# Forty unused matrix products behind the last product of a fused attention and token-mixer kernel

## The chip, the cores and the metric

The kernel runs on one core of one Trainium2 chip. The metric is the device time of one launch in microseconds, as the median of several executions. One further execution was recorded by the hardware profiler, and every row of a profile in this document comes from such a recorded execution. The engines are named as the profile names them: PE is TensorE (PEld its weight loads), DVE is VectorE, ACT is ScalarE, POOL is GpSimd, SP is SyncE. A "q" behind an engine's name marks its sequencer, which waits, branches and issues while the engine itself does no arithmetic.

## The reference

For x of 2048 tokens by 512 channels the kernel computes `g * a + (1 - g) * b`, where

- g is the sigmoid of the token's dot product with `gate_w`,
- a is softmax attention with 32 heads of 16 channels each (projections `wqkv` and `wo`),
- b is a mixer block across tokens: layer norm, `w1` (2048 to 1792), bias, gelu, `w2` (1792 to 2048), bias.

All values are float32.

## The kernel before, in words

The work has stages. First x is turned and split into two parts of reduced precision (a high and a low part, type fp32r), and the queries, keys and values are projected. Then comes the mixer's first layer. Then a long stage does the attention for 32 groups of heads; the mixer's second layer and most of the output projection are done in the same stage, product by product between the attention's products.

Three shapes of product on the array matter here.

- A score product (line 804, `s<-qs,ks`) uses 64 of the array's 128 rows and all 128 columns, with 512 moving columns, in fp32r. Two of them, one on each half of the rows, are issued next to each other.
- A value product (line 768, `av<-pt,v`) uses 128 rows and 17 columns, with 256 moving columns, in float32. Its output lies at partition 0, 32, 64 or 96, so four of them lie beside each other in the array's columns.
- The products of the output projection (line 887, `pa<-wo,o`) use 96 or 128 rows and all 128 columns, with 512 moving columns, in fp32r.

The last stage (lines 874 to 948) finishes eight tiles of the output. It has one PSUM bank for each tile, `pa[0]` to `pa[7]`, and runs in an order that is written out by hand (`manual_schedule`): each engine executes its instructions in the order of the code. The last pair of heads is normalised on DVE (`sums`, `hi`, `lo`, lines 903 to 910). TensorE then multiplies it into the even tiles (`last_pair(0, ...)`, line 917), then into the odd ones, and completes tiles 3, 5 and 7 with `others(*LATE)` (line 887). `finish(t, queue)` (lines 928 to 931) lets DVE add a finished bank to its row of the output, and lets SP or ACT store the row:

```python
        last_pair(1, parts, LATE)
        others(*LATE)
        for t, queue in ((1, nc.sync), (3, nc.scalar), (5, nc.sync), (7, nc.scalar)):
            finish(t, queue)
    end_ctx.close()
    att_ctx.close()

    far_off = nc.values_load(flag, min_val=0, max_val=H, skip_runtime_bounds_check_because="a count")
    with tc.If(far_off != 0):
```

Behind this stage every engine loads one number, `flag`, from memory into a register of its own sequencer (line 953), and branches on it (line 954). With these inputs the flag is zero, so every engine jumps over a long block that computes attention in a safer way. At the jump's target each engine waits for its own outstanding work, signals that it has arrived, and POOL collects these signals and releases all of them again; that is the end of the program (the rows of line 1027). In SP's list at the target stand waits for all transfers and for the other engines' counts.

The order of TensorE's instructions at the end is therefore: the products of line 917 for the odd tiles, twelve products of line 887, the load of the flag, the branch, and at its target the wait for its own products and the signal.

Of the kernel before, what the change touches and what calls it, by code (L numbers as in the profile page):

```python
# [21 lines left out]
P = 128  # L22
# [8 lines left out]
NB = 512  # L31
NQ = S // NB
VC = DH + 1
# [12 lines left out]
HALF = 64  # L46
# [12 lines left out]
def gated_mix(ctx: ExitStack, tc: tile.TileContext, a_x, a_wqkv, a_wo, b_w1, b_b1, b_w2, b_b2, gate_w, out):  # L59
    nc = tc.nc  # L60
# [277 lines left out]
    with tc.tile_pool(name="ln0", bufs=3, side="right") as ln:  # L338
# [18 lines left out]
        for b in range(ND):  # L357
# [9 lines left out]
            for n in range(NQ):  # L367
# [5 lines left out]
                if n % 2 == 0:  # L373
                    c = 2 * b + n // 2
# [39 lines left out]
    with tc.tile_pool(name="ln1", bufs=3, side="right") as ln, tc.tile_pool(name="gl", bufs=2, side="right") as gl:  # L414
# [29 lines left out]
        for f0, cs in order.items():  # L444
            n = min(NB, F - f0) // P
# [74 lines left out]
    QC = NB // 2  # L520
# [17 lines left out]
    def second_layer(t):  # L538

        box = []  # L540

        def step(fc, k):
            if fc == 0 and k == 0:
                box.append(ps_dn.tile([P, D], F32, name="dn"))
            if fc % 4 == 0 and k == 0:
                load_weight()
                box.append(ready.pop(0))
            at = slice(fc % 4 * P, (fc % 4 + 1) * P)
            hi, lo = (w[:, at] for w in box[-1])
            a, b = ((hi, u_hi), (hi, u_lo), (lo, u_hi))[k]  # L550
            last = fc == NF - 1 and k == 2
            return box[0], a, b[:, fc, :], fc == 0 and k == 0, last, (lambda: second_out(t, box[0])) if last else None

        return [(step, fc, k) for fc in range(NF) for k in range(3)]
# [59 lines left out]
    def o_matmuls(half, t, n, m):  # L614

        cols = slice(t % 8 * P, (t % 8 + 1) * P)
        for i in range(n, m):
            k, j = divmod(i, 3)
            hi, lo = (x[:, cols] for x in o_parts[half, k])
            a, b = ((hi, wo_hi), (hi, wo_lo), (lo, wo_hi))[j]  # L620
            yield a, b[: a.shape[0], k, :]
# [40 lines left out]
    def put(steps, at, sizes):  # L662
        for n in sizes:
            dense[at] = [steps.pop(0) for _ in range(n)]
            at += 1
        assert not steps
        return at
# [4 lines left out]
    def put_outputs(tiles, n, m, at, sizes=None):  # L672
        for t in tiles:
            steps, load = project(t, n, m)
            call(at - 1, load)
            at = put(steps, at, sizes or [m - n])
        return at

    def sizes_of(at, n, fours):

        sizes = [6] * n
        for i in [i for i in reversed(range(n)) if (at + i) % TWOS][:fours]:
            sizes[i] = 4
        return sizes
# [6 lines left out]
    first, at = steps[:28], put(steps[28:], 0, [8, 6])  # L691
    for t in range(NS):
        if t:
            at = put(second_layer(t), at, sizes_of(at, 9, 6) if t > 9 else sizes_of(at, 8, 3))
        if t == 7:
            call(at - 8, fetch_o, 0, 0)
            call(at - 5, fetch_o, 0, 1)
            at = put_outputs(range(NH), 0, 6, at)
        if t == 10:
            call(at - 8, fetch_o, 0, 2)  # L700
            call(at - 5, fetch_o, 0, 3)
            at = put_outputs(range(NH), 6, 12, at)
# [4 lines left out]
    at = put_outputs(range(NS - 3, NS), 0, 4, at)  # L707
    assert at == (NP + 12) * TWOS + 7
    call(at - 3, fetch_o, 1, 2)
    at = put_outputs(range(NH, NS - 3), 0, EARLY, at, [4, 4])  # L710
    at = put_outputs(range(NS - 3, NS), 4, EARLY, at)
# [9 lines left out]
    def column_halves(x):  # L721
        x = x.rearrange("p (i m c) -> p m i c", i=2, m=2)
        return x[:, 0], x[:, 1]
# [57 lines left out]
    with tc.manual_schedule(engines=engines):  # L781
# [3 lines left out]
        for n, (step, *args) in enumerate(first):  # L785
            if n and n % 12 == 0:
                split_weight(nc.vector.tensor_copy, nc.vector.tensor_tensor)
            ps, a, b, start, stop, done = step(*args)
# [27 lines left out]
        for grp in range(NG):  # L816
            at = [0, 0]
            for ph in range(2 * TWOS + 1):
# [45 lines left out]
                n = 2 if ph == 2 * TWOS and grp < NG - 1 else len(late)  # L864
# [8 lines left out]
    with (  # L873
        tc.tile_pool(name="ps_end", bufs=1, space=PSUM, reuse_waits="tile") as ps_end,
        tc.manual_schedule(engines=engines),
    ):
        pa = [ps_end.tile([P, D], F32, name=f"pa{t}") for t in range(8)]


        LATE = 3, 5, 7  # L880

        def others(*tiles, m=0, n=3 * ND):

            for t in tiles:
                mms = list(enumerate(o_matmuls(1, NH + t, EARLY, 3 * ND)))
                for i, (a, b) in mms[m:n]:
                    nc.tensor.matmul(pa[t], a, b, start=i == 0 and t not in LATE, stop=i == len(mms) - 1 and t in LATE)  # L887

        tiles = [end.tile([P, NB], dt, name=name) for name, dt in (("sums", F32), ("hi", F32R), ("lo", F32R))]
        sums, hi, lo = (column_halves(x) for x in tiles)  # L890
        last = column_halves(last_ot)
        totals = [column_halves(pa[t])[0] for t in (5, 7)]
        others(0, n=3)
        nc.tensor.matmul(totals[0], sums_of, last[0], start=True, stop=True)  # L894
        nc.tensor.matmul(totals[1], sums_of, last[1], start=True, stop=True)  # L895
        others(0, m=3)
        others(2, 4, 6)

        def low(m):
            nc.vector.tensor_tensor(lo[m], sums[m], hi[m].bitcast(F32), ALU.subtract)  # L900


        nc.vector.reciprocal(sums[0], totals[0])
        nc.vector.tensor_mul(sums[0], last[0], sums[0])
        nc.scalar.copy(hi[0], sums[0])
        nc.vector.reciprocal(sums[1], totals[1])
        low(0)
        nc.vector.tensor_mul(sums[1], last[1], sums[1])
        nc.vector.tensor_copy(hi[1], sums[1])
        low(1)  # L910

        def last_pair(m, parts, late=()):
            for n, (a, b) in enumerate(parts):
                for i in range(2):
                    for j in range(4):
                        t, at = 2 * j + m, slice(32 * j, 32 * j + DH)
                        nc.tensor.matmul(  # L917
                            pa[t],
                            a[m][at, i, :],
                            wq[b][at, i, :],  # L920
                            start=n == i == 0 and t in late,
                            stop=n == 2 and i == 1 and t not in late,
                        )

        def row_of(t):
            return rows[NH + t], g[:, NH + t : NH + t + 1], of[(NH + t) * P : (NH + t + 1) * P, :]

        def finish(t, queue):
            row, gate, dst = row_of(t)
            nc.vector.scalar_tensor_tensor(row, pa[t], gate, row, ALU.mult, ALU.add)  # L930
            queue.dma_start(dst, row)

        def scaled(t):
            res = end.tile([P, D], F32, name=f"res{t}")
            nc.scalar.activation(res, pa[t], AF.Copy, scale=row_of(t)[1])
            nc.gpsimd.tensor_tensor(row_of(t)[0], res, row_of(t)[0], ALU.add)

        parts = [(hi, 0), (hi, 1), (lo, 0)]
        last_pair(0, parts)
        others(1)  # L940
        scaled(2)
        for t, queue in ((0, nc.sync), (4, nc.scalar), (6, nc.sync)):
            finish(t, queue)
        nc.scalar.dma_start(row_of(2)[2], row_of(2)[0])
        last_pair(1, parts, LATE)
        others(*LATE)
        for t, queue in ((1, nc.sync), (3, nc.scalar), (5, nc.sync), (7, nc.scalar)):
            finish(t, queue)
    end_ctx.close()
    att_ctx.close()  # L950

# [2 lines left out]
    with tc.If(far_off != 0):  # L954
        with (
# [6 lines left out]
            for b in range(ND):  # L962
                with tc.For_i(0, P // DH, 1) as hi:
# [7 lines left out]
                    for t in range(NS):  # L971
# [4 lines left out]
                        m = pool.tile([P, 1], F32, name="m")  # L976
# [7 lines left out]
                        for n in range(NQ):  # L984
                            tp = ps_t.tile([P, NB // P, P], F32, name="tp")
                            for i in range(NB // P):
                                c = n * (NB // P) + i
# [3 lines left out]
                            for i in range(NB // P):  # L991
                                c = n * (NB // P) + i
                                nc.tensor.matmul(po, pt[:, i, :], vh[:, c, 0, :], start=c == 0, stop=c == NS - 1)
                        nc.vector.tensor_scalar_mul(og[:, t, ds(hi * DH + b * P, DH)], po, l)
            for t in range(NS):
# [6 lines left out]
                pa = ps_o.tile([P, NB], F32, name="po")  # L1002
# [28 lines left out]
```

## Time and profile before

| | us |
|---|---|
| median of 3 executions | 1308.36 (1308.08 to 1308.73) |
| the profiled execution, whole | 1307.55 |
| its span, from the first to the last instruction | 1305.8 |
| TensorE busy in the span | 1299.0 |
| start of the last product | 1299.79 |
| start of the last store's issue | 1300.99 |

A row of the timeline gives the start in microseconds from the start of the span, the duration, the engine, the source line, the operation, what it writes and reads, the shape (rows times columns of the array, then partitions times elements) and the number of instructions that are merged in the row. A row of the view of one source line gives the engine, the operation, the count, the least, median and greatest duration in nanoseconds, and the starts of the first and the last of them, to a tenth of a microsecond. A row of the chain of waits gives start and duration of one link. A row of the transfer queues gives packets, megabytes, and the time that the packets took as a share of sixteen engines over the window asked for, so that share times sixteen times the window is that time.

### The profile page before, as it was taken

The numbers are of one execution on the slowest core, as the hardware profiler recorded it, in microseconds if no ns is written. First come the engines' busy times: TensorE is split into PE (matmuls) and PEld (weight loads), VectorE is DVE, ScalarE is ACT, GpSimd is POOL, SyncE is SP. The second block draws the span as 40 slices with busy tenths as digits, with TensorE's granted clock in tenths as the row PEclk, the third lists the DMA queues.
The fourth block names the chain that finished last, engine by engine and source line by source line (L and its number), as shares of the span: only waits on it lengthen the run. The fifth ranks groups of instructions, "written<-read, shape, count | busy, mean of one in ns | idle before, by whom it ended". The sixth has DMA issues, their size and how long they took to land.

```text
span 1305.8 us, 32289 instructions
## 1 busy us (share of the span) xinstructions
PE 1299.0 (99%) x13282; PEld 764.3 (59%) x13282; DVE 403.9 (31%) x538; ACT 1090.6 (84%) x1248; POOL 200.0 (15%) x467
## 2 busy tenths in 40 slices
PE   9999999999999999999999999999999999999998
PEld 7888888886555555555555555555555555454444
DVE  5775361445121111122322111232111111233324
ACT  3443343448999999999999999999999999999994
POOL 0210244453101011011000111100010101100000
PEclk9999999999999999999999999999999999999999
DMA  4497643337443333334655443545433333365522
GB/s 129 144 308 275 229 117 97 97 88 148 75 86 66 62 75 84 69 75 90 126 113 121 82 76 72 120 115 118 79 67 63 74 62 77 75 123 115 112 64 74
DMA packets 93384, 138.41 MB, mean 106 GB/s; under 512 B 14293, under 2 KB 53355, under 8 KB 90156
## 3 DMA queue, kind: packets, MB, share of 16 engines
q1 hardware_dynamic: 92652, 135.20, 44.3%
q8 instruction: 107, 1.75, 0.6%
q10 hardware_dynamic: 576, 1.05, 0.2%
q14 instruction: 49, 0.40, 0.1%
HBM read 99.63 MB, written 36.56 MB: 104 GB/s over the span
## 4 chain that ended last, share of the span: by engine, by line
PE 99%; DVE 0%; issue 0%
PE av L768 37%; PE s L804 29%; PE acc L412 12%; PE acc L73 10%; PE dn L844 10%; PE pa L887 1%; PE acc L184 1%; PE dn L789 0%; PE acc L251 0%; PE acc L228 0%; PE pa L917 0%; DVE base L930 0%; PE pa L895 0%; PE pa L894 0%; DVE idle L223 0%; PE acc L210 0%
## 5 line engine op out<-in xcount | busy, mean ns | idle before, releaser
L813 ACT ACTIVATE pt<-s 128x1024 f32<-128x1024 f32 x1024 | 962.5, 1025 | 20.9 <-PE s L804 14.9
L804 PE MATMUL s<-qs,ks 64*128 64x512 f32 x2048 | 521.3, 420 | 0.0
L768 PE MATMUL av<-pt,v 128*17 128x256 f32 x8192 | 510.6, 381 | 0.0
L804 PEld LDWEIGHTS s<-qs,ks 64*128 64x128 f32 x2048 | 297.6, 184 | 207.6 <-ACT pt L813 182.8
L768 PEld LDWEIGHTS av<-pt,v 128*17 128x17 f32 x8192 | 205.3, 97 | 259.5 <-issue 119.2
L844 PE MATMUL dn<-u_hi,w_hi 64*128 64x512 f32 x428 | 179.6, 420 | 0.0
L844 PE MATMUL dn<-u_hi,w_lo 64*128 64x512 f32 x430 | 170.2, 396 | 0.0
L844 PE MATMUL dn<-u_lo,w_hi 64*128 64x512 f32 x430 | 170.1, 396 | 0.0
L66 POOL TENSOR_TENSOR w_lo<-w_raw,w_hi 128x512 fp32r<-128x512 f32 (+1 forms) x126 | 151.7, 1205 | 115.1 <-ACT w_hi L65 108.5
L848 POOL MEMSET token<- 1x1 f32 x320 | 29.9, 93 | 873.3 <-PE dn L844 704.1
L731 DVE COPY ot<-av 128x512 f32<-128x512 f32 x31 | 21.5, 692 | 344.9 <-PE av L768 344.9
L65 ACT CAST w_hi<-w_raw 128x512 fp32r<-128x512 f32 (+1 forms) x67 | 38.1, 569 | 79.6 <-PE acc L412 58.8
L742 DVE RECIPROCAL rt<-rt 128x512 f32<-128x512 f32 x31 | 104.0, 3353 | 1.1
L412 PE MATMUL acc<-h_hi,w_hi 128*128 128x512 f32 x224 | 87.1, 389 | 0.0
L412 PE MATMUL acc<-h_lo,w_hi 128*128 128x512 f32 x224 | 87.1, 389 | 0.0
L412 PE MATMUL acc<-h_hi,w_lo 128*128 128x512 f32 x224 | 87.1, 389 | 0.0
L65 DVE CAST w_hi<-w_raw 128x512 fp32r<-128x512 f32 (+1 forms) x61 | 23.5, 387 | 190.2 <-PE s L804 82.0
L844 PEld LDWEIGHTS dn<-u_lo,w_hi 64*128 64x128 f32 x430 | 79.5, 185 | 2.5 <-POOL token L848 0.2
L844 PEld LDWEIGHTS dn<-u_hi,w_lo 64*128 64x128 f32 x430 | 79.4, 185 | 2.6
L844 PEld LDWEIGHTS dn<-u_hi,w_hi 64*128 64x128 f32 x428 | 78.8, 184 | 2.2
L73 PE MATMUL acc<-xt_hi,wc_hi 128*128 128x512 f32 x128 | 49.8, 389 | 0.0
L73 PE MATMUL acc<-xt_lo,wc_hi 128*128 128x512 f32 x128 | 49.8, 389 | 0.0
(142 smaller groups left out, 1001.5 us busy)
## 6 DMA issues: line engine op xcount, KB each, us to landing
w_raw<-in_B_w_dram SPq DMA_DIRECT2D x96, 256.0 KB
ks<-kp SPq DMA_DIRECT2D x192, 128.0 KB
qs<-qp SPq DMA_DIRECT2D x256, 64.0 KB
qp<-pc SPq DMA_DIRECT2D x16, 768.0 KB
x<-in_A_x_dram SPq DMA_DIRECT2D x32, 256.0 KB
kp<-pc SPq DMA_DIRECT2D x16, 512.0 KB
w_raw<-in_B_w_dram SPq DMA_DIRECT2D x32, 128.0 KB
bp<-row SPq DMA_DIRECT2D x16, 256.0 KB
```

Of the source, the lines that this page charges most:

```text
L65: copy(hi, src)
L66: return sub(lo, src, hi.bitcast(F32), ALU.subtract)
L73: nc.tensor.matmul(ps, a, b, start=start and n == 0, stop=stop and n == last)
L184: nc.tensor.transpose(turns[t][:, k, :], xs[t][:, k * P : (k + 1) * P], ident)
L412: nc.tensor.matmul(p, a, b, start=first and k == 0, stop=last and k == 2)
L731: nc.vector.tensor_copy(ot, av)
L742: nc.vector.reciprocal(rt, rt)
L768: nc.tensor.matmul(av[32 * j : 32 * j + VC, i * QC : (i + 1) * QC], v[:, c, g % NP * 2 + i, :], pt[:, h * QC : (h + 1) * QC], start=added[ ...
L804: nc.tensor.matmul(s[:, m, :], kt[grp][rows, c * P : (c + 1) * P], qt[grp][rows, qb * NB : (qb + 1) * NB], start=True, stop=True,)
L813: nc.scalar.activation(pt, s, AF.Exp, scale=SCALE)
L844: mm = nc.tensor.matmul(ps, a[half], b[half], start=first and not second, stop=last and bool(second))
L848: fence = nc.gpsimd.memset(token, 0.0)
```

## The change

Behind the last `finish` of the last stage, and still inside its hand-written order, the changed kernel issues forty products. They read `sums`, `hi` and `lo`, which the stage has left in memory, and write the banks `pa[0]` and `pa[4]`, whose tiles have been read by DVE by then. Nothing reads what they write.

```diff
         for t, queue in ((1, nc.sync), (3, nc.scalar), (5, nc.sync), (7, nc.scalar)):
             finish(t, queue)
+        sums_t, parts_t = tiles[0], tiles[1:]
+        free = pa[0], pa[4]
+        def tile_of(r, c, rows_n, cols_n, n, a, b, m=None):
+            at = slice(r * rows_n, (r + 1) * rows_n)
+            m = m or cols_n
+            nc.tensor.matmul(
+                free[r][c * cols_n : c * cols_n + m, :n], a[at, c * cols_n : c * cols_n + m], b[at, :n], start=True, stop=True
+            )
+        def rounds(count, nr, n_cols, n, a, b, m=None):
+            for _ in range(count):
+                for c in range(n_cols):
+                    for r in range(nr):
+                        tile_of(r, c, P // nr, P // n_cols, n, a, b, m)
+        def score_slots(n):
+            rounds(n, 2, 1, NB, *parts_t)
+        def v_blocks(n, nr):
+            rounds(n, nr, 4, QC, sums_t, sums_t, VC)
+        score_slots(2)
+        v_blocks(1, 2)
+        score_slots(2)
+        v_blocks(1, 1)
+        v_blocks(1, 2)
+        score_slots(1)
+        for _ in range(2):
+            tile_of(0, 0, HALF, P, NB, *parts_t)
+            for c in range(4):
+                tile_of(1, c, HALF, 32, QC, sums_t, sums_t, VC)
     end_ctx.close()
     att_ctx.close()
```

`P` is 128, `HALF` 64, `NB` 512, `QC` 256 and `VC` 17. `score_slots(n)` issues n pairs of the score shape, one product on each half of the rows. `v_blocks(1, 1)` issues four products of the value shape; `v_blocks(1, 2)` issues eight, which use 64 rows each, so that the array is cut into two by four tiles. The last loop puts one product of the score shape on the upper half of the rows, and four of the value shape on the lower half, twice. Twelve products have the score shape and 28 a value shape. On TensorE the forty stand between the last product of line 887 and the load of the flag. The instructions of the other engines and their order are what they were.

## The prediction

> **What bounds the kernel now.** I read the page first, for the share of TensorE; then the last links of the chain of waits; then the timeline of the last microseconds; and last the views of the source lines 953, 954 and 1027, because behind the last product no engine is busy any more and the page shows nothing there. From the page and the chain:
>
> ```profile
> span 1305.8 us, 32289 instructions
> ...
> PE 1299.0 (99%) x13282; PEld 764.3 (59%) x13282; DVE 403.9 (31%) x538; ACT 1090.6 (84%) x1248; POOL 200.0 (15%) x467
> ```
>
> ```profile
> 1297.19 3.00 PE pa L887 x12
> 1300.19 0.02 issue
> 1300.21 0.75 DVE base L930
> ```
>
> TensorE is busy for 99% of the span, so forty more products look like forty more on the path. But the chain ends with a DVE row at 1300.96, and the span ends at 1305.8: for 4.8 us nothing is computed. What ends last there is not in the chain, which follows busy engines only. The timeline has the last product and the last store:
>
> ```profile
> 1299.79 0.39 PE L887 MATMUL pa<-wo_hi,o_lo 96*128 96x512 f32 x1
> ...
> 1300.99 0.34 ACTq L931 DMA_DIRECT2D out_dram<-base  x1
> ```
>
> The views of lines 953, 954 and 1027 have the sequencers:
>
> ```profile
> L953 PEldq TENSOR_LOAD <-flag x1: 772/772/772, 1296.1 to 1296.1; - x1
> ```
>
> ```profile
> L954 SPq EVENT_SEMAPHORE  x8: 17/17/17, 1303.8 to 1304.4; - x8
> ...
> L954 PEldq COMPARE_BRANCH  x1: 5028/5028/5028, 1297.0 to 1297.0; - x1
> L954 DVEq COMPARE_BRANCH  x1: 76/76/76, 1300.8 to 1300.8; - x1
> L954 SPq COMPARE_BRANCH  x1: 45/45/45, 1301.1 to 1301.1; - x1
> L954 ACTq COMPARE_BRANCH  x1: 54/54/54, 1301.9 to 1301.9; - x1
> L954 PEldq EVENT_SEMAPHORE  x1: 51/51/51, 1302.1 to 1302.1; - x1
> L954 DVEq EVENT_SEMAPHORE  x1: 21/21/21, 1304.2 to 1304.2; - x1
> L954 ACTq EVENT_SEMAPHORE  x1: 17/17/17, 1304.8 to 1304.8; - x1
> ```
>
> ```profile
> L1027 SPq DRAIN  x3: 7/7/7, 1305.0 to 1305.3; - x3
> L1027 POOLq EVENT_SEMAPHORE  x4: 17/17/17, 1305.0 to 1305.7; - x4
> ...
> L1027 PEldq DRAIN  x2: 8/8/8, 1302.2 to 1305.3; - x2
> ...
> L1027 ACTq DRAIN  x2: 8/8/8, 1304.9 to 1305.3; - x2
> ```
>
> The reader is to see four things. The jump costs DVE 1300.9 to 1304.2, SP 1301.1 to 1303.8 and ACT 1302.0 to 1304.8, that is 2.7 to 3.3 us each. The arrivals at the end (each engine's first DRAIN) are ACT's at 1304.9 and SP's at 1305.0; POOL collects them at 1305.0 and the span ends 0.8 us later. TensorE arrives at 1302.2, so it has **2.8 us of slack**. And its sequencer loads the flag at 1296.1, far ahead of the last product: the load does not wait for the array.
>
> **The change part by part.** Nothing is removed, and the other engines keep their instructions. So there is no mechanism for a gain; what is added stands on TensorE alone, and counts only as far as its arrival comes after 1305.0.
>
> *The array's time.* A float32 product counts twice: the code issues 4096 value products and the page has
>
> ```profile
> L768 PE MATMUL av<-pt,v 128*17 128x256 f32 x8192 | 510.6, 381 | 0.0
> ```
>
> So the 12 score products are 12 passes and the 28 value products 56, 68 in all. From the chain, then the timeline:
>
> ```profile
> 1283.48 1.42 PE av L768 x24
> 1284.90 0.66 PE s L804 x4
> ```
>
> ```profile
> 1287.42 0.13 PEld L768 LDWEIGHTS av<-pt,v 128*17 128x17 f32 x8 [0.50 <-ACT pt L813]
> 1287.97 0.19 PEld L887 LDWEIGHTS pa<-wo_hi,o_lo 128*128 128x128 f32 x1 [0.42 <-issue]
> ```
>
> Four score products cost 0.66 us with the change of tiling behind them, two I take at half, 0.33. Eight value passes cost 0.55 up to the next shape; 24 cost 1.42, so four more cost (1.42 - 0.55) / 4 = 0.22, and the change of tiling about 0.55 - 2 x 0.22 = 0.11. Four value passes at a time is what this rate means, since one lasts 381 ns. The value shape on half the rows is in no row. Bound from below: eight at a time, as column tiles run four at a time and row halves two at a time, 0.55 for its 16 passes. Four at a time would be 0.55 + 2 x 0.22 = 0.99. From above: one after another, 16 x 0.22 + 0.11 = 3.63. I take eight at a time, because both ways of sharing are in the two rows. In order: 0.66 (4 passes), 0.55 (16), 0.66 (4), 0.55 (8), 0.55 (16), 0.33 (2), and twice 0.33 + 0.55 (9 each), **5.06 us**; four at a time 5.94. It starts at 1299.79 + 0.22 + 0.11 = 1300.12 and ends at 1305.2 (1306.1). The first two products wait until DVE has read `pa[0]` and `pa[4]`, the first two of
>
> ```profile
> 1294.61 2.06 DVE L930 SCALAR_TENSOR_TENSOR base<-pa,g,base 128x512 f32<-128x512 f32 x3
> ```
>
> which is done by 1294.61 + 2/3 x 2.06 = 1296.0; the wait costs nothing, and only TensorE's own work is queued behind it. If the array were all that counts, TensorE would arrive at 1305.3 and cost 0.3.
>
> *The sequencer's time.* The forty stand ahead of the flag's load, and behind the load come the jump and the arrival. How far ahead of the array does the sequencer get? At the load, 1296.1, these were still to come or running (busy time of one window, the count in brackets, then a row of the timeline):
>
> ```profile
> 1296.11:1300.40 4.29, 4.06 (x32) 1.00 0.94 334
> ```
>
> ```profile
> 1296.55 0.64 PE L917 MATMUL pa<-wq,lo 16*128 16x512 f32 x8
> ```
>
> At most 32 passes, at least these 8 and the 12 of line 887: 20 to 32, and I take 24. So with 68 added the load is reached when about 44 have started, 48 and 36 at the ends. All three lie in the fifth block (passes 33 to 48), which opens at 1300.12 + 0.66 + 0.55 + 0.66 + 0.55 = 1302.54. The 44th is in its second group: **1302.8** (four at a time: 1303.4). [...]
>
> *The jump.* From load to branch is 1297.0 - 1296.1 = 0.9. The branch took 5.0 on TensorE, against 2.7 to 3.3 elsewhere. The transfer queues tell why: three windows, 1297.3 to 1297.4, 1299.6 to 1299.7 and, for DVE, 1301.9 to 1302.1, hold the start of one fetch of instructions each.
>
> ```profile
> q8 instruction: 1, 0.02, 63.4%
> ```
>
> ```profile
> q8 instruction: 1, 0.02, 59.4%
> ```
>
> ```profile
> q14 instruction: 1, 0.01, 23.9%
> ```
>
> Share times 16 times window: 1.01, 0.95 and 0.76 us. DVE's fetch starts 1.0 us after its branch, and DVE goes on 1304.2 - 1302.7 = 1.5 after the fetch. TensorE's second fetch ends at 1300.6 and it goes on 1.4 later, at 1302.0: that is the target's. It starts 2.6 after the branch, not 1.0, because, as I read it, an ordinary fetch was under way until 1298.3. In the changed kernel that ordinary fetch comes at the same place in the code, 136 instructions ahead of the new place of the jump, and is long over. So the branch costs 1.0 + 0.95 + 1.4 = **3.4**; SP's 2.7 is the end below, 5.0 the end above.
>
> *The sum.* Load 1302.8, branch 1303.7, target 1307.1, signal 0.1 later 1307.2, end 0.8 later 1308.0. Against 1305.8 that is **2.2 us** later. The profiled execution is 1307.55 us long, 1.75 more than its span; with 2.2 it would be 1309.8. It lies 0.8 under the median, and the difference carries over: 1308.36 + 2.2 = **1310.6 us**. With four at a time 2.8 us and 1311.2; with a branch of 2.7, 1.5 us and 1309.9.
>
> **The rivals.**
>
> *The tail hides it.* If the sequencer can run much further ahead than 24, the jump is over before the array is done: 0.3 us, 1308.7 (1.2 us and 1309.6 with four at a time). For it: no row shows a limit. Against it: 20 to 32 at a moment when it had no wait left to hold it. 0.12.
>
> *The jump costs 5.0 again: slower.* If the long branch is a property of TensorE, or another fetch is under way at the new place, TensorE's arrival moves by 1.6 more: 3.8 us, 1312.2, with four at a time 1312.8. It decides from a branch of 3.8 us on, where the sum passes 2.6. For it: the only jump of TensorE in the trace took 5.0. Against it: the second fetch, which explains the difference. 0.18.
>
> *Passes in strict order: slower.* If no pass may start before the one ahead of it, the second pass of a product on a tile holds back the next tile, and each value product costs 0.22: the blocks are 0.66, 1.87, 0.66, 0.99, 1.87, 0.33 and twice 1.32, the load falls at 1304.30 + 6 x 0.22 = 1305.6, and the sum is 5.0 us, 1313.4. Against it: 24 value passes, 12 products, took 1.42 and not 2.64. 0.12. [...]
>
> *Half-row value tiles one after another.* The load falls at 1306.9 + 2.6 = 1309.6 and the sum is 9.0 us, 1317.4. Against it: both ways of sharing are seen. 0.05.
>
> *The change does nothing*, because the unused products are dropped: 1308.4. Against it: they stand in TensorE's list. 0.03.
>
> **How the numbers follow.** The forecast, 1309.9 to 1311.2 with 1310.6 likeliest, has 0.50. With the hidden case and the 5.0 us branch it holds 0.80, so the range is 1308.7 to 1312.8. About 0.2%, 2.6 us, is what a measurement of this kernel can tell from no change; the bound is at 1311.0, and I put 0.08 of the forecast's 0.50 beyond it. Slower by more than that: 0.08 + 0.18 + 0.12 + 0.05 = 0.43. Within it: 0.42 + 0.12 + 0.02 = 0.56. Faster: 0.01, left from the case without effect.
>
> **What would show it.** In the changed profile TensorE's load of the flag should stand about 3.0 us after the start of the last product of line 887 (before, 3.7 us ahead of it); its branch should take about 3.4 us; its first DRAIN should be the last, about 7.4 us after that product's start, with SP's still at about 5.2; and the added passes should take about 5.1 us. I am wrong if SP's or ACT's DRAIN is still the last one, if the branch again takes 5 us, or if the sixteen passes on half the rows take much more than 0.6 us.

## The result, and the profile after

| | before | after |
|---|---|---|
| median of 4 executions, us | 1308.22 (1307.82 to 1308.73) | 1314.30 (1314.13 to 1314.84) |
| profiled execution, us | 1307.55 | 1314.44 |
| its span, us | 1305.8 | 1312.7 |

The changed kernel is **6.1 us slower**: the ratio is 1.0047 (95%: 1.003 to 1.0064). The forecast was 1310.6, and the range ended at 1312.8.

From the page of the changed kernel, its head; then the last links of its chain of waits:

```profile
span 1312.7 us, 32425 instructions
...
PE 1304.5 (99%) x13350; PEld 766.4 (58%) x13350; DVE 404.4 (31%) x538; ACT 1090.9 (83%) x1248; POOL 198.8 (15%) x467
```

```profile
1298.27 3.00 PE pa L887 x12
1301.26 5.24 PE pa L958 x68
```

The 68 added passes are there (13350 - 13282), with a weight load each, and they take 5.24 us. But the chain stops at 1301.26 + 5.24 = 1306.50 and the span goes on to 1312.7: for 6.2 us no engine computes. Before, that stretch was 4.8 us. What fills it has to be read in the rows of the sequencers. The lines have moved down: the load of the flag is line 988, the branch 989, the meeting at the end 1062. The first fence has the load, the second the branch and the signal, the third the meeting:

```profile
L988 PEldq TENSOR_LOAD <-flag x1: 483/483/483, 1304.9 to 1304.9; - x1
```

```profile
L989 ACTq COMPARE_BRANCH  x1: 54/54/54, 1303.0 to 1303.0; - x1
...
L989 PEldq COMPARE_BRANCH  x1: 3734/3734/3734, 1305.5 to 1305.5; - x1
...
L989 PEldq EVENT_SEMAPHORE  x1: 51/51/51, 1309.3 to 1309.3; - x1
```

```profile
L1062 SPq EVENT_SEMAPHORE  x10: 17/28/3251, 1305.8 to 1312.6; - x10
L1062 POOLq EVENT_SEMAPHORE  x4: 17/17/17, 1309.6 to 1312.6; - x4
...
L1062 SPq DRAIN  x3: 7/7/7, 1309.5 to 1312.4; - x3
...
L1062 ACTq DRAIN  x2: 8/8/8, 1305.8 to 1312.4; - x2
L1062 PEldq DRAIN  x2: 8/8/8, 1309.5 to 1312.4; - x2
L1062 ACTq EVENT_SEMAPHORE  x2: 17/17/17, 1309.7 to 1312.6; - x2
L1062 DVEq EVENT_SEMAPHORE  x2: 21/21/21, 1309.7 to 1312.6; - x2
L1062 PEldq EVENT_SEMAPHORE  x2: 51/51/51, 1312.3 to 1312.6; - x2
```

The reader is to see two delays, one behind the other. First, TensorE's arrival (its first DRAIN) is now the last: 1309.5, while ACT arrived at 1305.8, and SP waits 3.25 us for it. Second, the meeting itself has become long. Each engine's two EVENT_SEMAPHORE rows here are the taking of the release and the last signal. ACT and DVE take the release at 1309.7, and **TensorE takes it at 1312.3**, 2.6 us after them. The last signals wait for that. The same rows of the kernel before, for SP's longest wait there, 28 ns, and for the release, which TensorE took with the others:

```profile
L1027 SPq EVENT_SEMAPHORE  x10: 17/28/28, 1304.5 to 1305.7; - x10
...
L1027 ACTq EVENT_SEMAPHORE  x2: 17/17/17, 1305.2 to 1305.7; - x2
...
L1027 PEldq EVENT_SEMAPHORE  x2: 51/51/51, 1305.2 to 1305.7; - x2
```

What holds TensorE between 1309.5 and 1312.3 is in the transfer queues. Two windows of the changed kernel, 1306.0 to 1306.6 and 1309.85 to 1310.0 (q8 I take for the queue that fetches TensorE's instructions: over most of the kernel before it has one packet for 256 of TensorE's rows, as counted in the next section):

```profile
q8 instruction: 1, 0.02, 13.7%
```

```profile
q8 instruction: 1, 0.02, 41.7%
```

Share times 16 times window: the first fetch, the only one between the branch and the arrival and so, as I read it, that of the jump's target, took 1.32 us. It starts at 1306.45, 0.94 after the branch. The second took 1.00 us. It starts at 1309.91, after the arrival, and TensorE goes on 1.37 us after its end. Before, there was such a second fetch as well, in the window 1302.9 to 1303.1:

```profile
q8 instruction: 1, 0.02, 34.8%
```

It took 1.11 us and cost nothing, because TensorE had arrived at 1302.2 and was released only at 1305.2.

All further times in the tail are counted from the start of the last product of line 887 (1299.785 before, 1300.866 after), because that start varies between executions of the same code: it lies from 1299.87 to 1300.73 in the experiments. The 1.08 us between the two profiles at that point lie ahead of the change and are scatter, not its effect. From that start to the end of the span it is 5.99 us before and **11.81 after: 5.81 us more**, which is the 6.1 us of the medians but for 0.3.

| after the start of the last product of line 887, us | before | predicted | after |
|---|---|---|---|
| last added pass starts | | about +5 | +5.26 |
| TensorE loads the flag | -3.68 | +3.0 | +4.06 |
| TensorE branches | -2.80 | +3.9 | +4.65 |
| TensorE arrives (first DRAIN) | +2.44 | +7.4 | +8.59 |
| ACT and DVE take the release | +5.4 | | +8.9 |
| TensorE takes the release | +5.41 | | +11.42 |
| end of the span | +5.99 | +8.2 | +11.81 |

### The profile page after: what moved, and what is told of

It reads as the page before. It is cut to its first block, busy times and chain, and to the rows that moved or that the text cites. A ratio compares the mean times of both kernels' runs of the same rounds, so it can differ in the third digit from the quotient of the medians.

```text
span 1312.7 us, 32425 instructions
## 1 busy us (share of the span) xinstructions
PE 1304.5 (99%) x13350; PEld 766.4 (58%) x13350; DVE 404.4 (31%) x538; ACT 1090.9 (83%) x1248; POOL 198.8 (15%) x467
## 3 DMA queue, kind: packets, MB, share of 16 engines
q8 instruction: 107, 1.75, 0.6%
q10 hardware_dynamic: 576, 1.05, 0.2%
## 4 chain that ended last, share of the span: by engine, by line
PE 99%; DMA 1%; SPq 0%; DVE 0%; issue 0%
PE av L768 37%; PE s L804 27%; PE acc L412 11%; PE dn L844 11%; PE acc L73 10%; PE pa L887 1%; PE acc L184 1%; PE acc L251 0%; PE pa L958 0%; DMA ks<-kp 0%; DMA qs<-qp 0%; PE acc L228 0%; PE pa L917 0%; PE pa L894 0%; PE pa L895 0%; SPq L131 0%
```

## The experiments

Before them I counted TensorE's instructions in the program as built. The change adds 136 (two for a pass; the page's 32425 - 32289 agrees). The profile's row for q8, 107 fetches and 1.75 MB before, makes 16.4 KB a fetch. From the fetch at 20.3 us to the one at 1297.4 there are 104 fetches, and TensorE has 13188 products, 13187 weight loads and some 260 rows of its sequencer, which makes 256 instructions a fetch. I assume that these blocks of 256 are counted from the first instruction on. Then in the changed kernel one block ends exactly behind TensorE's arrival, and the wait for the release is the first instruction of the next. Before, some 139 instructions lay between the target and the end of its block. This place of the block's end is an estimate from the program, and no trace shows it, because the skipped block does not run; e1, e5 and e9 are its tests.

So the theory, an inference from the two fetches above, was: behind the jump TensorE has the target's block alone, and where the block ends behind the arrival it has to fetch the next before it can take the release. Whenever an expectation numbers this theory, it is the first; its numbered rivals put the late release down to something other than the place of the code, and foresee that it stays when the code is moved. Ratios are to the kernel before, run beside each experiment (medians 1308.43 for the first four, 1308.58 for the next four, 1308.47 for the last).

**e1: the changed kernel, its end moved by code that is never executed.** The products stand in the block that the jump skips; they move the target by 31 instructions.

```diff
+            spare = ps_o.tile([P, NB], F32, name="po")
+            for _ in range(16):
+                nc.tensor.matmul(spare, wo_lo[:, 0, :P], wo_hi[:, 0, :], start=True, stop=True)
             og = pool.tile([P, NS, D], F32, name="og", bufs=1)
```

> The changed kernel with 16 more products (31 instructions net on TensorE) inside the block that every engine jumps over; nothing of it is executed, only the addresses behind the jump move. Tail means from the start of the last product of line 887 to the end of the span: 5.99 us before (1299.79 to 1305.78), 11.81 after (1300.87 to 1312.67). Theory 1: 2.6 us of the loss are a second fetch of instructions, because the end of a 16 KB block of TensorE's code falls by chance between its signal of arrival and its wait for the release; moved by 31 instructions the target and all that follows lie in one block, the second stall goes, tail 9.2 us, time about 1311.7. Theory 2: TensorE has to wait for a second fetch after every jump, wherever it lands; tail 11.8 us, time 1314.3. Theory 3: the products themselves cost it; 1314.3 as well.

Measured: 1311.34 us (ratio 1.0023, 1.0014 to 1.0033), tail 9.16. The view of the line of the meeting, now 1065:

```profile
L1065 SPq DRAIN  x3: 7/7/7, 1308.4 to 1308.7; - x3
...
L1065 PEldq DRAIN  x2: 8/8/8, 1308.4 to 1308.8; - x2
...
L1065 DVEq EVENT_SEMAPHORE  x2: 21/21/21, 1308.7 to 1309.2; - x2
L1065 PEldq EVENT_SEMAPHORE  x2: 51/51/51, 1308.7 to 1309.2; - x2
```

The late arrival is still there (+8.31), but TensorE takes the release with the others (+8.58) and the span ends 0.85 us after the arrival. The second fetch starts at +8.78, when nothing waits for it. The theory holds: 2.65 us of the tail went with 16 products that no engine executes. Of these, 2.37 us lie behind the arrival (3.22 us from it to the end in the changed kernel, 0.85 here); 0.28 us lie ahead of it, in a shorter branch (3.45 us against 3.73), and nothing ties them to the block's end.

**e2: the changed kernel, the same products with 8 moving columns.** Same number of instructions, so the same place of the block's end.

```diff
-                free[r][c * cols_n : c * cols_n + m, :n], a[at, c * cols_n : c * cols_n + m], b[at, :n], start=True, stop=True
+                free[r][c * cols_n : c * cols_n + m, :8], a[at, c * cols_n : c * cols_n + m], b[at, :8], start=True, stop=True
```

> The changed kernel with the forty products cut to 8 moving columns each (the rest of their columns is left out; nobody reads them). The count of instructions and all addresses stay. The array's stretch was 5.1 us and should shrink to 2 or 3. Theory 1 (the sequencer can run only some 13 products ahead of the array, and the jump starts when it reaches it): the load of the flag comes 1.5 to 2.5 us after the start of the last product of line 887 instead of 4.06, the arrival moves with it, the stall at the block's end stays, tail 9.2 to 10.3 us, time 1311.7 to 1312.8. Rival: the sequencer's own pace sets the load (136 instructions in 7.8 us since its last wait, 57 ns each): load still at 4.06, tail 11.8, time 1314.3.

Measured: 1312.15 us (1.0031, 1.0018 to 1.0044), tail 10.12. The added passes now end their starts at +2.21, 3.05 us earlier, and the arrival comes at +6.88, only 1.71 earlier, after a load that took 0.97 and a branch of 3.77. At the load as many products are still to start as in the changed kernel, 13. In these two kernels, then, how far the sequencer ran ahead went with the place in the list, not with time. The release is taken at +9.74, while ACT and DVE take it at +7.15: from the arrival to the release it is 2.86 us, as in the changed kernel (2.83), so the second delay is as long with a short array stretch.

```profile
L1062 PEldq DRAIN  x2: 8/8/8, 1307.6 to 1310.6; - x2
L1062 ACTq EVENT_SEMAPHORE  x2: 17/17/17, 1307.9 to 1310.8; - x2
...
L1062 PEldq EVENT_SEMAPHORE  x2: 51/51/51, 1310.5 to 1310.8; - x2
```

**e3 and e4: the changed kernel and the kernel before without the flag and the jump.** Both leave out the safer attention, which these inputs don't use. The diff, cut to its first lines, is the same for both:

```diff
-    far_off = nc.values_load(flag, min_val=0, max_val=H, skip_runtime_bounds_check_because="a count")
-    with tc.If(far_off != 0):
...
```

> The changed kernel without the load of the flag, the branch and the skipped block (left out: the safer attention for inputs that need it; these do not). Theory 1: with no jump there is no fetch behind it, and TensorE arrives when its products are done, 5.5 to 5.7 us after the start of the last product of line 887; tail about 6.4 us. Theory 3 (the products cost the 5.8 us by themselves): tail still 5.8 us above that of the kernel before without its jump.

> The kernel before without the load of the flag, the branch and the skipped block (left out as in the run beside it). All theories: the end is set by the last store's landing, 3.8 us after the start of the last product of line 887, and SP's list of waits; tail 4.5 to 5.0 us, time about 1307.2. Theory 1: the forty products cost 1.4 to 1.9 us between this run and the one beside it; theory 3: 5.8.

Measured: 1308.52 us with the forty products (1.0001, 0.9991 to 1.001), tail 6.50; 1306.64 without them (0.9988, 0.9978 to 0.9997), tail 4.76. The forty products cost 1.88 us by the medians, 1.74 in the tail. Two rows show where: in e3, then e4, TensorE's two DRAINs, of which the first now waits for the array:

```profile
L1008 PEldq DRAIN  x2: 13/836/1658, 1304.1 to 1306.2; - x2
```

```profile
L973 PEldq DRAIN  x2: 13/2058/4103, 1296.6 to 1304.7; - x2
```

In e3 it ends at +5.71, and SP has waited 1.56 us for it; in e4 it ends at +0.44, 3.56 us before SP's own arrival. So the same array time that costs 1.7 us here goes with 5.8 us where a load and a jump stand behind it.

**e5: the kernel before, its end moved as far as the change moves it.** Products in the skipped block as in e1, 68 of them (135 instructions).

```diff
+            for _ in range(68):
+                nc.tensor.matmul(spare, wo_lo[:, 0, :P], wo_hi[:, 0, :], start=True, stop=True)
```

> The kernel before with 68 products (135 instructions net on TensorE) inside the skipped block and nothing added that is executed; the target of TensorE's jump then lies within one instruction of where it lies in the changed kernel, at the end of a 16 KB block. Theory 1 (the second fetch stalls TensorE, and costs only what comes after the other engines' arrival): TensorE arrives at 2.4 us after the start of the last product of line 887, its second fetch is done near 5.5, the others release it at 5.4; tail 6.0 to 6.2 us, time within 0.3 us of the kernel before. Rival (the place of the target costs by itself, whatever else TensorE does): 2.6 us more, tail 8.6, time 1311.

Measured: 1307.99 us (0.9998, 0.9989 to 1.0007), tail 6.27. The block's end alone costs next to nothing while TensorE arrives early (+2.24): its DRAIN after the release comes at +6.00, where the others have theirs at +5.8. In these runs the delay needs both, a late arrival and the block's end behind it.

**e6 and e7: one shape alone.** All seven calls of the change are replaced by one: 34 passes of the score shape, then 64 passes of the value shape on half the rows.

```diff
+        score_slots(17)
```

```diff
+        v_blocks(4, 2)
```

> One part of the change alone: 17 pairs of the score shape (34 passes) in place of the forty. The array's stretch is 17 x 0.235 + 0.1 = 4.1 us. The target lies 68 instructions away from the block's end, so no second stall is due. If the sequencer always runs 13 passes ahead, the load of the flag comes when the 21st has started, 2.7 us after the start of the last product of line 887; tail = load + 0.6 + 3.45 + 0.2 + 0.85 = 7.8 us, time 1310.2. If 13 came from the mix of tilings at the end of the forty and the lead without it is 20 (before: 24), the load comes at 1.7, tail 6.8 us, time 1309.3.

> One part alone: four rounds of the eight half-row value tiles (64 passes) in place of the forty. The array's stretch is 8 x 0.22 + 0.1 = 1.9 us. No second stall is due (the target lies 8 instructions off). With a lead of 13 passes the load comes at 1.65 us after the start of the last product of line 887, tail 6.75 us, time 1309.1; with a lead of 24 at 1.2, tail 6.3 us, time 1308.7. If half-row value tiles were costly in themselves, the stretch would be far above 1.9.

Measured: e6 1310.36 us (1.0012, 1.0003 to 1.0021), tail 7.45; e7 1309.50 us (1.0008, 0.9999 to 1.0017), tail 6.83, both within 0.2% of the kernel before. In e6 the load comes when 20 products are still to start, which the expectation had as its second case; what it had not is 0.98 from load to branch and a branch of 3.57, which put the arrival at +6.60. That the time is near the 1310.2 of the first case is therefore chance. In e7, 16 are still to start. By the count, in neither does the block's end fall in the meeting, and TensorE takes the release with the others. The chain of e7 has its 64 passes:

```profile
1300.31 1.88 PE pa L958 x64
```

**e8: the kernel before, the flag loaded earlier.** The load moves ahead of the products of line 917.

```diff
+        far_off = nc.values_load(flag, min_val=0, max_val=H, skip_runtime_bounds_check_because="a count")
         parts = [(hi, 0), (hi, 1), (lo, 0)]
...
-    far_off = nc.values_load(flag, min_val=0, max_val=H, skip_runtime_bounds_check_because="a count")
```

> The kernel before with the load of the flag moved ahead of the last products and stores (the branch stays where it is, so the same value is tested). ACT and SP then branch right behind their last store instead of 0.55 us later: tail 5.4 to 5.5 us instead of 5.99, time about 0.5 us below the kernel before, which is less than this measurement can tell. If the load was not on the path (SP's waits for the stores' landing end the kernel), tail 6.0.

Measured: 1308.74 us (1.0002, 0.9993 to 1.0011), tail 6.12. ACT and SP branch about 0.6 us earlier and ACT arrives at +4.77, but SP arrives at +5.3, no earlier than before (+5.17). SP's eight rows behind its branch, of 17 ns each, are spread from 1303.8 to 1304.8, and before from 1303.8 to 1304.4; I read the longer stretch as a wait for the last store's landing. By that reading the stores end the kernel in this profile; the time shows no gain.

**e9: e7 with 7 instructions more in the skipped block.** Four products there, so that the block's end falls in the meeting again, by the count one instruction later than in the changed kernel: behind the taking of the release.

```diff
+            for _ in range(4):
+                nc.tensor.matmul(spare, wo_lo[:, 0, :P], wo_hi[:, 0, :], start=True, stop=True)
```

> The run with the four rounds of value tiles alone (tail 6.83 us, 1309.5 us), with 4 more products (7 or 8 instructions on TensorE) inside the skipped block; nothing more is executed. By the instruction count this puts the end of the 16 KB block back to where TensorE waits for its release, as in the changed kernel. Theory 1: the second fetch stalls TensorE again, 2.6 us more: tail 9.4 to 9.6 us, time about 1312.1. Rival (the gain of the padded run came from something else, such as a luckier fetch): tail 6.8 us, 1309.5.

Measured: 1311.08 us (1.0021, 1.0011 to 1.003), tail 9.07 against 6.83. The meeting of e7, then of e9:

```profile
L1053 ACTq DRAIN  x2: 8/8/8, 1305.0 to 1306.2; - x2
L1053 PEldq DRAIN  x2: 8/8/8, 1305.9 to 1306.3; - x2
...
L1053 PEldq EVENT_SEMAPHORE  x2: 51/51/51, 1306.2 to 1306.7; - x2
```

```profile
L1056 ACTq DRAIN  x2: 8/8/8, 1305.4 to 1306.6; - x2
L1056 PEldq DRAIN  x2: 8/8/8, 1306.2 to 1309.0; - x2
...
L1056 PEldq EVENT_SEMAPHORE  x2: 51/51/51, 1306.5 to 1309.2; - x2
```

The arrival is at the same place (+5.97 and +6.01) and the release is taken at once in both (+6.24 and +6.28). In e9 the next instruction, the second DRAIN, comes only at 1309.0, where ACT has its own at 1306.6. The window 1306.6 to 1306.7 of e9 has the fetch, 0.622 x 16 x 0.1 = 1.0 us:

```profile
q8 instruction: 1, 0.02, 62.2%
```

It starts at +6.47, and TensorE goes on 1.38 us after its end, as in the changed kernel (1.37). Seven instructions that are never executed cost 2.24 us of the tail; the stop moved by the one instruction that the count gave. The expectation had 9.4 to 9.6 us and 1312.1, too much: the instruction behind the block's end comes 2.83 us after the arrival, as in the changed kernel, but here the release has been taken by then, and 0.23 us are left to the end in place of 0.39. The medians show only 1.6 us between e7 and e9, because an execution of e7 has 2.57 us outside its span (median), against about 1.8 in every other kernel; the median spans, 1307.1 and 1309.35, differ by 2.25.

## Why the prediction was wrong

*What bounds the end: right.* It was not TensorE's busy time but the meeting, and TensorE's sequencer had to reach load, jump and signal behind the added products. Its arrival became the last one and SP's long wait shows it.

*The array's time: right.* Predicted 5.06 us, chain 5.24. Sixteen passes of the value shape on half the rows run eight at a time, in the prediction's sense: eight start side by side, and the next eight 0.21 to 0.23 us later, though a pass lasts 376 to 390 ns in the rows. The timeline has such a block, the next shape's start, and so 0.58 us for it:

```profile
1301.86 0.65 PE L958 MATMUL pa<-sums 64*17 64x256 f32 x16
...
1302.44 0.73 PE L958 MATMUL pa<-lo,hi 64*128 64x512 f32 x4
```

The rivals "strict order" (1.87 for such a block) and "one after another" (3.63) fall; that the first of them gave 1313.4, the nearest number to the result, is chance. (The 1317.4 us of "one after another" is too high by the prediction's own terms: it lets the eight passes on all rows cost 1.87 too, for which it had 0.55, and without that it is about 1316.)

*The lead of the sequencer: a term mis-sized.* I took 24 passes, from a count of 20 to 32 at one place of the kernel before. At the load of the changed kernel, the window from there on has

```profile
1304.93:1306.60 1.67, 1.57 (x18) 0.41 (x17) 0.00 (x0) 0.00 (x0) 0.00 (x0) 1.00 0.09 25
```

18 passes to come or running, 13 of them still to start, so the load fell at +4.06 and not at +3.0. Counted in the same way (still to start), it was 24 in the kernel before, 20 in e6, 16 in e7, 13 in e2. The lead differed from one mixture of shapes to the next; one number carried over from another mixture was wrong by 1.05 us. The 13 lie below the whole range of 20 to 32 that I had counted.

*The jump: right in size.* Predicted 0.9 from the load and 3.4 for the branch; 0.59 and 3.73 measured here, 3.45 to 3.77 in the five experiments whose jump stands behind added products. The rival of 5.0 us again is wrong. My reason for it is not supported, though. I had put the long branch of the kernel before down to an ordinary fetch that was under way. In e5 the branch took 4.83 us, and from it to its end one fetch is recorded, the target's, in the window 1297.1 to 1301.9. A second window, 1299.5 to 1299.6, holds its start, 2.5 us after the branch:

```profile
q8 instruction: 1, 0.02, 1.3%
```

```profile
q8 instruction: 1, 0.02, 60.5%
```

No other fetch is recorded that it could have waited for. In the kernel before the products and the stores of the last stage run between the branch and the start of the target's fetch, 1296.99 to 1299.66: TensorE is busy for all of these 2.67 us, and the DMA share is 1.01. In e5 the two queues of the stores take a share of 1.00 from 1297.1 to 1299.0. Running products alone are not the cause: in the changed kernel TensorE is busy for the whole of the time from the branch to the fetch too, and it is 0.94 us. Transfers alone do not make a branch of that length either: in e7 the DMA share is 0.70 from 1301.42 to 1303.00, the products are over at 1302.2, and the branch at 1302.0 took 3.67 us; in e2 it is 0.58 from 1302.55 to 1304.00, the products are over at 1303.1, and the branch at 1303.6 took 3.77 us. Both together, or something else, was not tried and stays open.

*"End 0.8 later": the step that failed.* The prediction took the time from the last arrival to the end of the span, 0.8 us, as fixed, because in the kernel before it was so. There ACT and SP were the last, and TensorE had 2.8 us in which to fetch its next block unseen. I made TensorE the last to arrive and still counted on that cover. From the arrival to the end it took 3.22 us in place of 0.8. I had even asked which ordinary fetch the new place of the jump would meet, but ahead of the jump and not behind its target. None of the three signs by which the prediction said it would be wrong came: TensorE's DRAIN is the last, the branch took 3.7 us and not 5, and the sixteen passes took 0.6. The end of the span was not among the signs.

The 5.81 us of the tail therefore come apart like this, by the differences of tails: 3.17 for TensorE's later arrival (e1 against the kernel before, 9.16 - 5.99), and 2.65 between the changed kernel and e1 (11.81 - 9.16), of which 2.37 are the stop at the block's end and 0.28 a longer branch. The 1.74 us between e3 and e4 are not a part of the 3.17: without the jump SP arrives at +4.0, with it at +5.2. An estimate from these rows: had the array alone counted, TensorE would have arrived at +5.71 as in e3, some 0.5 us behind SP; the rest of the 3.17 is the load and the jump that stand behind the products. The prediction had the later arrival at 2.2, and the mis-sized lead accounts for the difference; with it alone e1 is at 1311.34, inside the range. The block's end was in no rival, and put the time beyond the range. It is shown twice, by taking it away (e1) and by bringing it back elsewhere (e9), and e5 shows that it needs the late arrival.

What stays open besides the long branch: what sets the lead of 13, 16, 20 or 24 products. No version that keeps the safe path beats the kernel before; e4 is 1308.43 - 1306.64 = 1.8 us faster, and leaves that path out.

## What to carry to other kernels

Work behind the last product is free only as far as the engine that gets it has slack at the program's end (TensorE's 2.8 us here), and everything that its sequencer still has to do behind that work (a load, a jump, a signal, the taking of a release) has to be counted in its own rows, since the busy rows and the chain show none of it. When an engine becomes the last to arrive, each cost that its slack covered comes due, so ask what it did in that slack. Behind a jump the place of the code counted here: where an engine arrived last and a block of its instructions ended within its last few steps, this cost 2.2 to 2.4 us here, and some products in code that is never executed moved it away.

## What the runs showed of the hardware that I had not expected

- A taken jump on TensorE costs 3.45 to 3.77 us behind the added products, whether they still run or not, and 4.3 to 5.0 in the three kernels (before, e5, e8) that jump beside the last stage's products and stores. The fetch of the target itself takes 1.32 us of it in the changed kernel, 0.95 before and 0.97 in e5, and starts 0.94 us after the branch in the first, 2.7 and 2.5 in the other two.
- In the kernel before, the changed kernel, e1 and e9 the second fetch behind the jump, which I take for the next block's, starts only after TensorE's arrival: 0.7 us in the kernel before, 0.45 to 0.5 in the other three. In the changed kernel and e9 the instruction that I place behind the block's end comes 1.37 and 1.38 us after that fetch's end, 2.83 us after the arrival.
- Eight float32 tiles of 64 rows and 17 columns run beside each other: in the changed kernel eight start within 0.05 us and last 376 to 390 ns each, and e7 took 1.88 us for 64 passes, 0.03 us each, where four tiles of 128 rows took 0.22 / 4 = 0.055 a pass in the kernel before.
